# Back-to-back score halves and two shared PSUM banks in an attention and mixture-of-experts kernel

## The chip, the cores and the metric

The kernel runs on one core of a Trainium2 chip. The metric is the device time of one execution in microseconds (us); lower is better. The engines are named as in the profile: PE (TensorE; PEld is its weight loading), DVE (VectorE), ACT (ScalarE), POOL (GpSimd) and SP (SyncE, which only issues DMAs here).

## The reference

Sliding-window attention with a linear position bias, 8 sequences of 576 tokens, 8 heads of 64, then a mixture of experts in which each token takes only its best expert.

```python
# q, k, v: [8, 8, 576, 64] fp32
scores = q @ k^T / 8 - slope[h] * |i - j|        # 0 <= i - j < 128, else masked
attn   = exp(scores - max) ;  attn /= attn.sum() + 1e-9
x      = (attn @ v) as [4608, 512]               # tokens x (heads * 64)
logits = x @ w_gate                              # [4608, 8]
e      = argmax(logits) ;  g = softmax(logits)[e]
out    = g * (relu(x @ w1[e]) @ w2[e])           # w1 [8, 512, 1024], w2 [8, 1024, 512]
```

## The kernel before, in words

**Two stages.** The attention stage works through 36 chunks of 128 query rows, all 8 heads each, and writes rows and gates to a scratch tensor `xd` in HBM; a small routing computation goes on beside it. The expert stage then gathers each expert's rows from `xd` and runs the two layers. This study is about the attention stage.

**A chunk** passes through ten pieces of work, numbered `k` in `do`:

| k | what it is | engines |
|---|---|---|
| 0, 4 | scores of the first, the second four heads (`scores`): bias by a bf16 matmul, then q times k, into the two-bank tile `s0_ps` or `s1_ps`; in 64x64 tiles of the array | PE |
| 2, 5 | `weigh` of the first, the second four heads: `copy_predicated` folds the window, `tensor_reduce` takes the maximum, four exponentials with their sums go to `pe` | DVE, then ACT |
| 1, 6 | `transposes` of the first, the second four heads into one PSUM bank, a copy of it to `pT`, two masks by `affine_select` | PE, ACT, POOL |
| 7, 8 | value products (`av`) into one PSUM bank `x_ps` | PE |
| 9 | `copy_x`: that bank to `xT` | ACT |
| 3 | `rows`: `xT` times identity and gate weights into `r_ps` (two banks), scaled to `x_sb` by DVE, written to `xd`; the logits `lg` | PE, DVE, SP |

Below, S0 and S1 stand for the two score halves, T0 and T1 for the two transposes, A for the value products and R for the rows' matmuls.

**What sets the order.** Nothing is scheduled by a planner here: inside `manual_schedule` every engine runs its instructions in the order in which the code issues them. That order comes from steps. `LAGS[None][k]` says how many steps after step 4·chunk piece `k` is issued, so four steps are one period, in which one chunk's worth of each piece is issued, from five different chunks. Inside a step the pieces are sorted by the key in `step`. Before, a period c is, for PE: S0 of chunk c, T0 of c-1, R of c-4, T1 of c-1, S1 of c, A of c-2.

**Chunks differ.** In each nine chunks the first and the sixth begin a sequence (called narrow below: only one key block, so their scores are 128 instead of 192 columns wide, they have no fold, and A has half as many matmuls); the fifth is a tail of two sequences, whose A before is issued in two halves, one on each side of S1. So periods whose chunk c-2 is narrow (7, 11, 16, 20, 25, 29 and so on) have half an A.

**PSUM.** Eight banks: four for `s0_ps` and `s1_ps`, one for the transposes (`ps_t`), one for the value products (`ps_x`), two for `r_ps`.

**Routing.** After each group of chunks (`GROUPS`) a generator `route` goes through five stages, one in each period: 1 the maximum and the one-hot of the expert; 2 small matmuls on PE that count ranks, put into spare columns of `r_ps` by `spare`, and DVE work on them; 3 and 4 DVE work; 5 index matmuls on PE, again into `r_ps`. They are issued at the end of a step with s % 4 == 3, right behind A; for the groups at chunks 21, 27 and 30 `PACE` names the steps itself. Stage 3 of the group at chunk 21 also calls `shift_late`, which has one small matmul into `r_ps`.

**Weights.** From step `FETCH` on, `round_half` (a cast on ACT) and `rest_half` (a subtraction on POOL) split the first expert's weights, half a block a period.

Of the kernel before, what the change touches and what calls it, by code (L numbers as in the profile page):

```python
# [9 lines left out]
F32 = mybir.dt.float32  # L10
# [6 lines left out]
PSUM = bass.MemoryType.PSUM  # L17
# [14 lines left out]
def keep(tc, ins):  # L32
    return ins if HELD[0] else tc.keep_in_program_order(ins)


def attention(ctx, tc, st, qT, kT, v, iw, load_c2, chunk_done, chunks, begun):
# [5 lines left out]
    ptp = ctx.enter_context(tc.tile_pool(name="a_pt", bufs=2))  # L42
    xp = ctx.enter_context(tc.tile_pool(name="a_x", bufs=2))
    ps_s = ctx.enter_context(tc.tile_pool(name="ps_s", bufs=1, space=PSUM))
    ps_t = ctx.enter_context(tc.tile_pool(name="ps_t", bufs=1, space=PSUM))
    ps_x = ctx.enter_context(tc.tile_pool(name="ps_x", bufs=1, space=PSUM))
    ps_r = ctx.enter_context(tc.tile_pool(name="ps_r", bufs=1, space=PSUM))
    st["ps_x"], st["ps_t"], st["ptp"] = ps_x, ps_t, ptp

    batch = {}  # L50
    blocks = {}
# [2 lines left out]
    def score_banks():  # L54
        turns.append(turns.pop(0))
        return turns[-1]
# [60 lines left out]
                                          start=True, stop=True))  # L117

    def warm_up(n):
        w_ps = ps_x.tile([128, 512], F32, name="x_ps")  # L120
        for _ in range(n):
            keep(tc, nc.tensor.matmul(out=w_ps, lhsT=warm[:, 0:128], rhs=warm, start=True, stop=True))

    def early(op):
        bank = score_banks()[:, 0] if op not in "zog" else None
        st["early"][0](op, bank if bank is None else bank.rearrange("p a b -> p (a b)"))

    k0 = load_k(0, (0, KCUT, 320, S))
    next(k0)
# [68 lines left out]

    def transposes(subs, g, pe, pT):
        m, tail = subs[0][1] // 4, is_tail(subs)  # L200
        t_ps = ps_t.tile([128, 4, 128], F32, name="t_ps")
        for j in range(4):
            nc.tensor.transpose(out=t_ps[:, j, :], in_=pe[:, 4 * g + j, :], identity=ident)  # L203
        cut = lambda kb: pT[:, kb, 4 * g:4 * g + 4, :]
        nc.scalar.copy(out=cut(1), in_=t_ps)
        if tail:
            part = lambda ap: ap.rearrange("p h (a q) -> p h a q", a=2)
            pat = lambda k: [[0, 4], [0, 2], [k, 64]]
        else:
            part = lambda ap: ap  # L210
            pat = lambda k: [[0, 4], [k, 128]]
        if m > 0:
            nc.gpsimd.affine_select(out=part(cut(0)), in_=part(cut(1)), pattern=pat(-1), base=0,
                                    channel_multiplier=1, compare_op=ALU.is_gt, fill=0.0)
            nc.gpsimd.affine_select(out=part(cut(1)), in_=part(cut(1)), pattern=pat(1), base=0,
                                    channel_multiplier=-1, compare_op=ALU.is_ge, fill=0.0)
# [53 lines left out]
    live, pes, sums, pTs, xTs, xps, second = {}, {}, {}, {}, {}, {}, {}  # L270

    def copy_x(ch):
        xTs[ch] = xp.tile([128, NP, 128], F32, name="xT", bufs=3)
        nc.scalar.copy(out=xTs[ch], in_=xps.pop(ch))

    def do(k, ch):
        if k == 9:
            return copy_x(ch)
        subs = chunks[ch]
        if k in (0, 4):  # L280
            if k == 0:
                pes[ch] = pp.tile([128, H, 128], F32, name="pe")
                sums[ch] = small.tile([128, H], F32, name="rsum", bufs=8)
            live[ch] = scores(subs, k // 4)
        elif k in (2, 5):
            second[ch] = weigh(k // 3, pes[ch], sums[ch], *live.pop(ch), later=k == 5 and ch == len(chunks) - 1)
        elif k == 1:
            pTs[ch] = ptp.tile([128, 2, H, 128], F32, name="pT")
            transposes(subs, 0, pes[ch], pTs[ch])
            if second.get(ch):  # L290
                second.pop(ch)()
        elif k == 3:
            rows(ch, subs, xTs.pop(ch), sums.pop(ch))
        elif k == 6:
            transposes(subs, 1, pes.pop(ch), pTs[ch])
        elif k == 7:
            xps[ch] = ps_x.tile([128, NP, 128], F32, name="x_ps")
            av(subs, pTs[ch], xps[ch], range(NP // 2))
        else:
            av(subs, pTs.pop(ch), xps[ch], range(NP // 2, NP))  # L300
            if len(lags(ch)) < 10:
                copy_x(ch)

    def step(s):
        st["step"] = s
        if s == 0:
            begun(0)
        if s == 12:
            begun(1)
        for f, b, m in ahead.get(s, ()):  # L310
            f(b, m)
        for k, ch in sorted(plan.get(s, ()), key=lambda x: (1.5 if x[0] == 9 else 4.5 if x == (6, s // 4 - 1) and s % 4 == 2 else x[0], x[1])):
            do(k, ch)
        if s < len(WU) - 1:
            warm_up(WU[s + 1])
        for k in list(st["stages"]):
            if k[1] <= s and (s in PACE[k[2]] if k[2] in PACE else s % 4 == 3):
                k[1] = s + 1
                if next(k[0], k) is k:
                    st["stages"].remove(k)  # L320
        n, i = divmod(s - FETCH, 8)
        if 0 <= n < 7 and i in (0, 3, 4, 7):
# [14 lines left out]
        step(s)  # L337


LAGS = {None: (0, 4, 0, 17, 2, 2, 5, 11, 11, 12)}  # L340
LAGS.update({ch: (0, 4, 0, 17, 2, 2, 6, 11, 11, 12) for ch in range(3)})
LAGS.update({ch: (0, 4, 0, 17, 2, 2, 5, 9, 11, 12) for ch in (4, 13, 22, 31)})
LAGS.update({33: (0, 4, 0, 15, 2, 2, 5, 11, 11), 34: (0, 4, 0, 13, 2, 2, 5, 10, 10), 35: (0, 4, 0, 10, 2, 2, 5, 8, 8)})
HAND = 152
HANDS = lambda nc: {x.engine for x in (nc.tensor, nc.vector, nc.scalar, nc.gpsimd, nc.sync)}
# [9 lines left out]
PP = 3  # L355
OS = (3,)
WN = 7
FETCH = 57
WV = (0, 1)
KCUT = 128  # L360
LAST = 2
# [5 lines left out]
TT = 6  # L367
# [58 lines left out]

def spare(st, k, n):
    if st["step"] >= FREE_T:
        return st["ps_t"].tile([128, 4, 128], F32, name="t_ps")[:, k, 0:n]
    return st["r_ps"][:, k, XW:XW + n]  # L430


# [104 lines left out]
def route_last(tc, st, lg, ch, groups):  # L537
# [8 lines left out]
    key = rp.tile([128, E], F32, name="l_key", bufs=1)  # L546
# [9 lines left out]
    rest = [r for r, *_ in st["stages"]]  # L556
    st["stages"].clear()
    st["warm"](0)
    bank = st["ps_x"].tile([128, 512], F32, name="x_ps")
    rank = bank[:, 0:E]  # L560
    nc.tensor.matmul(out=rank, lhsT=tri[:, 0, :], rhs=oh, start=True, stop=False)
    nc.tensor.matmul(out=rank, lhsT=tri[:, 1, :], rhs=prev, start=False, stop=True)
    for r in rest:
# [8 lines left out]
    s = st["rank"][:, ch:ch + 1]  # L572
# [8 lines left out]
    st["warm"](1)  # L581
    for r in rest:
        list(r)
    ip = st["ps_x"].tile([128, 512], F32, name="x_ps")[:, 0:E * TT]
    for t, lp in lps.items():
        for k in range(2):
            nc.tensor.matmul(out=ip[:, E * t:E * t + E], lhsT=lp, rhs=rr[:, k, :], start=(k == 0), stop=(k == 1))
# [676 lines left out]
```

## Time and profile before

| | us |
|---|---|
| time, median of 3 runs (650.93 to 651.36) | 651.24 |
| time of the profiled execution | 651.34 |
| its span, first to last instruction | 649.5 |
| PE busy in the span | 635.6 |
| of it, in the 429.10 us from 211.90 to 641.00 (experts) | 429.10 |
| of it, in the 172.64 us from 17.00 to 189.64 (chunks 3 to 32) | 170.20 |
| DVE, ACT, POOL busy in those 172.64 us | 135.24, 141.24, 105.71 |

The granted clock of TensorE is 0.996 over the span and 1.00 in both stretches. A busy PE is not the same as a PE at its peak: its matmuls overlap and their modelled ends cover short waits, so in the attention stage the distances between the starts of matmuls say more than the busy time does.

### The profile page before, as it was taken

Reading aid. Unit: us, or ns where it says so; the run is one execution under the profiler, and the core shown is the slowest. Engines: PE = TensorE matmul, PEld = TensorE weight load, DVE = VectorE, ACT = ScalarE, POOL = GpSimd, SP = SyncE. Lnnn points to the kernel's source line nnn. Section 1 sums busy time; section 2 is a strip of 40 time slices with the busy share of each in tenths; the row PEclk is TensorE's granted clock in tenths of the full one; section 3 lists DMA queues with packets and bytes.
Section 4 is the critical chain, followed back from the end, with each engine's and each line's share of the span. In section 5 each row is a group of like instructions: output and inputs, shape, how many; then the busy total and the mean of one; then the engine's idle time right before and its main releaser. Section 6 shows DMA issues by size and latency. Waiting matters only on the chain.

```text
span 649.5 us, 15087 instructions
## 1 busy us (share of the span) xinstructions
PE 635.6 (98%) x5683; PEld 541.4 (83%) x5683; DVE 389.8 (60%) x974; ACT 316.2 (49%) x963; POOL 302.2 (47%) x414
## 2 busy tenths in 40 slices
PE   8999999999999999999999999999999999999995
PEld 4878878787887988988889889898898888888884
DVE  5568888969889786545543663565455456355411
ACT  6877778888777424433342333334233333433311
POOL 5644657768555141066317616733760750580202
PEclk9999999999999999999999999999999999999998
DMA  8958887897645243473526325433542542543101
GB/s 312 282 162 205 208 238 233 210 292 191 196 105 116 67 154 92 163 248 102 191 98 182 103 77 174 124 89 127 156 107 96 171 124 77 179 120 132 65 0 62
DMA packets 57646, 97.91 MB, mean 151 GB/s; under 512 B 11669, under 2 KB 31765, under 8 KB 56674
## 3 DMA queue, kind: packets, MB, share of 16 engines
q1 hardware_dynamic: 49090, 76.89, 39.4%
q0 software_dynamic: 8336, 19.76, 10.7%
q8 instruction: 46, 0.75, 0.5%
q14 instruction: 30, 0.25, 0.1%
q10 hardware_dynamic: 144, 0.26, 0.1%
HBM read 77.91 MB, written 18.98 MB: 149 GB/s over the span
## 4 chain that ended last, share of the span: by engine, by line
PE 68%; DVE 0%; ACT 0%; issue 0%; POOLq 0%; POOL 0%; ACTq 0%
PE y_ps L877 32%; PE l_ps L681 30%; PE s_ps L681 2%; PE x_ps L231 1%; PE r_ps L241 1%; PE x_ps L642 1%; PE y_ps L837 1%; PE t_ps L203 1%; PE x_ps L837 0%; PE s_ps L171 0%; ACT pe L190 0%; PE s_ps L642 0%; PE s_ps L162 0%; POOLq L1030 0%; PE l_ps L653 0%
## 5 line engine op out<-in xcount | busy, mean ns | idle before, releaser
L684 ACT ACTIVATE hh<-l_ps 128x336 fp32r<-128x336 f32 (+7 forms) x104 | 46.5, 447 | 203.2 <-PE l_ps L681 202.8
L688 DVE SCALAR_TENSOR_TENSOR hl<-l_ps,hh 128x336 fp32r<-128x336 f32 (+7 forms) x104 | 52.1, 501 | 151.0 <-ACT hh L684 150.8
L661 POOL DMA_INDIRECT xg<-xd,od_idx x112 | 116.7, 1042 | 35.1 <-issue 34.5
L190 ACT ACTIVATE pe<-s_ps,nmax 128x128 f32<-128x128 f32 x288 | 102.4, 376 | 32.0 <-DVE nmax L184 22.8
L877 PE MATMUL y_ps<-wh,hh 128*128 128x512 f32 (+5 forms) x280 | 110.9, 396 | 0.0
L877 PE MATMUL y_ps<-wh,hl 128*128 128x512 f32 (+5 forms) x280 | 110.4, 394 | 0.0
L877 PE MATMUL y_ps<-wl,hh 128*128 128x512 f32 (+5 forms) x280 | 110.3, 394 | 0.0
L865 POOL DMA_INDIRECT out<-y,od_pidx x33 | 34.8, 1055 | 151.7 <-ACT y L883 145.2
L969 DVE TENSOR_TENSOR wl<-w_raw,wh 128x512 fp32r<-128x512 f32 x114 | 73.9, 690 | 31.7 <-ACT wh L965 29.6
L681 PE MATMUL l_ps<-xh,wh 128*128 128x304 f32 (+9 forms) x416 | 81.7, 318 | 0.0
L681 PE MATMUL l_ps<-xh,wl 128*128 128x304 f32 (+9 forms) x416 | 81.0, 317 | 0.0
L681 PE MATMUL l_ps<-xl,wh 128*128 128x304 f32 (+9 forms) x416 | 80.8, 316 | 0.0
L681 PEld LDWEIGHTS l_ps<-xh,wh 128*128 128x128 f32 x416 | 68.1, 189 | 8.3 <-issue 1.2
L681 PEld LDWEIGHTS l_ps<-xh,wl 128*128 128x128 f32 x416 | 66.4, 189 | 1.9
L681 PEld LDWEIGHTS l_ps<-xl,wh 128*128 128x128 f32 x416 | 66.3, 189 | 1.7
L231 PE MATMUL x_ps<-pT,v_sb 128*64 128x128 f32 (+2 forms) x1152 | 66.4, 265 | 0.1
L231 PEld LDWEIGHTS x_ps<-pT,v_sb 128*64 128x64 f32 (+1 forms) x1152 | 57.0, 137 | 9.8 <-issue 5.2
L877 PEld LDWEIGHTS y_ps<-wh,hl 128*128 128x128 f32 (+5 forms) x280 | 51.4, 184 | 13.6
L965 ACT CAST wh<-w_raw 128x1024 fp32r<-128x1024 f32 x57 | 59.5, 1044 | 4.3 <-DMA w_raw<-w 4.3
L190 ACT ACTIVATION_READ_ACCUMULATOR pe<-s_ps,nmax 128x1 f32 x288 | 61.5, 214 | 0.0
L877 PEld LDWEIGHTS y_ps<-wl,hh 128*128 128x128 f32 (+5 forms) x280 | 51.6, 184 | 11.3
L877 PEld LDWEIGHTS y_ps<-wh,hh 128*128 128x128 f32 (+5 forms) x280 | 51.4, 184 | 10.3 <-ACT hh L684 0.4
(221 smaller groups left out, 957.4 us busy)
## 6 DMA issues: line engine op xcount, KB each, us to landing
w_raw<-w SPq DMA_DIRECT2D x64, 512.0 KB, 3.8
q_sb<-qT SPq DMA_DIRECT2D x39, 256.0 KB, 5.4
xd<-x_sb SPq DMA_DIRECT2D x32, 258.0 KB, 5.0
v_sb<-v SPq DMA_DIRECT2D x32, 256.0 KB, 5.0
k_sb<-kT SPq DMA_DIRECT2D x7, 1152.0 KB, 9.3
w_n<-w SPq DMA_DIRECT2D x4, 1024.0 KB, 6.2
xg<-xd,od_idx POOLq DMA_INDIRECT x112, 3.1
xd<-x_sb SPq DMA_DIRECT2D x8, 129.0 KB, 4.3
```

Source lines behind the costliest of these rows:

```text
L190: nc.scalar.activation(out=pe[:, h, :], in_=s_ps[:, c, n, lo:lo + 128], func=AF.Exp, bias=nmax[:, 2 * c + n:2 * c + n + 1], scale=1.0, acc ...
L203: nc.tensor.transpose(out=t_ps[:, j, :], in_=pe[:, 4 * g + j, :], identity=ident)
L231: nc.tensor.matmul(out=x_ps[64 * c:64 * c + 64, p, q], lhsT=blocks["v", b, m - 1 + kb][0:kk, D * h:D * h + D], rhs=pT[0:kk, kb, h, q], sta ...
L241: nc.tensor.matmul(out=r_ps[:, p, 0:XW], lhsT=xT[:, p, :], rhs=iw_sb[:, p, :], start=True, stop=True)
L661: ins = tc.nc.gpsimd.indirect_dma_start(out=g[:, s], out_offset=None, in_=parts, in_offset=bass.IndirectOffsetOnAxis(ap=idx[:, s], axis=0),)
L681: nc.tensor.matmul(out=ps, lhsT=a[:, 128 * d:128 * d + 128], rhs=b[:, d], start=(k == 0), stop=(k == 11))
L684: nc.scalar.activation(out=hh, in_=ps, func=AF.Relu)
L688: nc.vector.scalar_tensor_tensor(out=hl, in0=ps, scalar=0.0, in1=hh.bitcast(F32), op0=ALU.max, op1=ALU.subtract)
L865: ins = nc.gpsimd.indirect_dma_start(**kw).ins
L877: nc.tensor.matmul(out=ys[t][0:n], lhsT=a[:, tl], rhs=b[:, 512:1024], start=(f == 0 and k == 0), stop=(f == 7 and k == 2))
L965: keep(tc, nc.scalar.copy(out=wh, in_=raw))
L969: keep(tc, eng.tensor_tensor(out=wl[:, sl], in0=raw[:, sl], in1=wh.bitcast(F32)[:, sl], op=ALU.subtract))
```

## The change

Five edits, all in the attention stage.

1. For chunks 3 to 32 (`PAIRED`) both score halves are issued in the first step of a period (lags 0 and 0), T0 in the second with the first `weigh` behind it (lags 5 and 1), T1 in the third, then the second `weigh`, then the rows (lags 6, 2, 14; the order inside the step is set by `rank`).
2. The rows come 14 steps after the chunk's first step in place of 17, for chunks 0 to 2 too.
3. Transposes and value products take turns in one pool of two banks (`ps_b`); the warm-up matmuls and the last spare columns use it too.
4. Both halves of a tail chunk's value products are issued in one step (the lag 9 is gone).
5. `copy_x` comes first behind S0 in its step; `FETCH` is 56 in place of 57.

```diff
-    ps_t = ctx.enter_context(tc.tile_pool(name="ps_t", bufs=1, space=PSUM))
-    ps_x = ctx.enter_context(tc.tile_pool(name="ps_x", bufs=1, space=PSUM))
+    ps_b = ctx.enter_context(tc.tile_pool(name="ps_b", bufs=2, space=PSUM))
     ps_r = ctx.enter_context(tc.tile_pool(name="ps_r", bufs=1, space=PSUM))
+    st["bank"] = bank = lambda: ps_b.tile([128, 4, 128], F32, name="b_ps")
...
     def transposes(subs, g, pe, pT):
-        t_ps = ps_t.tile([128, 4, 128], F32, name="t_ps")
+        t_ps = bank()
...
-            live[ch] = scores(subs, k // 4)
+            live[ch, k // 4] = scores(subs, k // 4)
...
-            xps[ch] = ps_x.tile([128, NP, 128], F32, name="x_ps")
+            xps[ch] = bank()
...
+    def rank(k, ch, s):
+        if ch in PAIRED and k in (5, 6):
+            return 2.4 if k == 6 else 2.6
+        return 0.5 if k == 9 else 4.5 if (k, ch) == (6, s // 4 - 1) and s % 4 == 2 else k
...
-        for k, ch in sorted(plan.get(s, ()), key=lambda x: (1.5 if x[0] == 9 else 4.5 if x == (6, s // 4 - 1) and s % 4 == 2 else x[0], x[1])):
+        for k, ch in sorted(plan.get(s, ()), key=lambda x: (rank(*x, s), x[1])):
...
-LAGS = {None: (0, 4, 0, 17, 2, 2, 5, 11, 11, 12)}
-LAGS.update({ch: (0, 4, 0, 17, 2, 2, 6, 11, 11, 12) for ch in range(3)})
-LAGS.update({ch: (0, 4, 0, 17, 2, 2, 5, 9, 11, 12) for ch in (4, 13, 22, 31)})
+PAIRED = range(3, 33)
+LAGS = {None: (0, 5, 1, 14, 0, 2, 6, 11, 11, 12)}
+LAGS.update({ch: (0, 4, 0, 14, 2, 2, 6, 11, 11, 12) for ch in range(3)})
...
-FETCH = 57
+FETCH = 56
```

The line numbers of the changed kernel are 1 to 6 higher than those before. First place: PE in period 11, a period with half an A. Before (line 171 is the q-times-k part of S0 and S1, 203 the transposes, 241 the rows, 231 the value products):

```order
L171 MATMUL s0_ps_107<-k_sb_565,q_sb_763 64x192 x8
L203 MATMUL t_ps_1189<-c2_sb_64,pe_1076 128x128 x4
L241 MATMUL r_ps_1208<-iw_sb_114,xT_1097 128x144 x4
L203 MATMUL t_ps_1218<-c2_sb_64,pe_1076 128x128 x4
...
L171 MATMUL s1_ps_108<-k_sb_565,q_sb_763 64x192 x8
L231 MATMUL x_ps_1250<-pT_1090,v_sb_1072 64x128 x8
```

The same period in the changed kernel:

```order
L172 MATMUL s0_ps_104<-k_sb_574,q_sb_772 64x192 x8
...
L172 MATMUL s1_ps_105<-k_sb_574,q_sb_772 64x192 x8
L204 MATMUL b_ps_1221<-c2_sb_64,pe_1093 128x128 x4
L204 MATMUL b_ps_1238<-c2_sb_64,pe_1093 128x128 x4
L242 MATMUL r_ps_1256<-iw_sb_111,xT_1204 128x144 x4
L232 MATMUL b_ps_1266<-pT_1121,v_sb_1089 64x128 x8
```

S1 has moved up to S0, T1 to T0, and the rows now stand directly ahead of the value products.

Second place: ACT in one period. Before, the second line's `xT` copy and the cast `wh` lie between copies of the transposes (`pT`) and exponentials (`pe`):

```order
L205 COPY pT_1837<-t_ps_1838 128x512
L274 COPY xT_1846<-x_ps_1803 128x512
L190 ACTIVATE pe_1823,rsum_1824<-s0_ps_107,nmax_1849 128x128 x4
L205 COPY pT_1837<-t_ps_1869 128x512
L981 CAST wh_1779<-w_raw_1433 128x512
L190 ACTIVATE pe_1823,rsum_1824<-s1_ps_108,nmax_1894 128x128 x4
```

In the changed kernel:

```order
L275 COPY xT_1859<-b_ps_1820 128x512
L986 CAST wh_1771<-w_raw_1431 128x512
L206 COPY pT_1876<-b_ps_1877 128x512
L191 ACTIVATE pe_1845,rsum_1846<-s0_ps_104,nmax_1886 128x128 x4
L206 COPY pT_1876<-b_ps_1893 128x512
L191 ACTIVATE pe_1845,rsum_1846<-s1_ps_105,nmax_1902 128x128 x4
```

The `xT` copy and the cast have moved ahead of both `pT` copies, so the run from the first `pT` copy to the last exponential holds nothing else.

Third place: PE in period 31, where `PACE` puts routing stage 2 into the third step. Before, S1 (its last rows are the first two) lies between the rows and the first rank matmul (`tri` is a triangle of ones):

```order
L241 MATMUL r_ps_3361<-iw_sb_114,xT_3237 128x144 x4
L203 MATMUL t_ps_3372<-c2_sb_64,pe_3214 128x128 x4
...
L171 MATMUL s1_ps_108<-k_sb_2479,q_sb_2916 64x192 x2
L171 MATMUL s1_ps_108<-k_sb_2920,q_sb_2918 64x192 x2
L459 LDWEIGHTS tri_169
L459 MATMUL r_ps_3361<-oh_3296,tri_169 128x48
```

In the changed kernel:

```order
L204 MATMUL b_ps_3366<-c2_sb_64,pe_3223 128x128 x4
L204 MATMUL b_ps_3382<-c2_sb_64,pe_3223 128x128 x4
L242 MATMUL r_ps_3400<-iw_sb_111,xT_3351 128x144 x4
L465 LDWEIGHTS tri_166
L465 MATMUL r_ps_3400<-oh_3306,tri_166 128x48
```

The rank matmuls now follow the rows at once, in the same tile `r_ps`; the single matmul of `shift_late` stands likewise behind the rows of period 32.

More of the change, by code (lines that the diff above doesn't have):

```diff
@@ L44, in attention @@
     ps_s = ctx.enter_context(tc.tile_pool(name="ps_s", bufs=1, space=PSUM))
-    ps_t = ctx.enter_context(tc.tile_pool(name="ps_t", bufs=1, space=PSUM))
-    ps_x = ctx.enter_context(tc.tile_pool(name="ps_x", bufs=1, space=PSUM))
+    ps_b = ctx.enter_context(tc.tile_pool(name="ps_b", bufs=2, space=PSUM))
     ps_r = ctx.enter_context(tc.tile_pool(name="ps_r", bufs=1, space=PSUM))
-    st["ps_x"], st["ps_t"], st["ptp"] = ps_x, ps_t, ptp
+    st["bank"] = bank = lambda: ps_b.tile([128, 4, 128], F32, name="b_ps")
+    flat = lambda ap: ap.rearrange("p a b -> p (a b)")
+    st["ptp"] = ptp
     batch = {}
@@ L119, in warm_up @@
     def warm_up(n):
-        w_ps = ps_x.tile([128, 512], F32, name="x_ps")
+        w_ps = flat(bank())
         for _ in range(n):
@@ L124, in early @@
     def early(op):
-        bank = score_banks()[:, 0] if op not in "zog" else None
-        st["early"][0](op, bank if bank is None else bank.rearrange("p a b -> p (a b)"))
+        half = score_banks()[:, 0] if op not in "zog" else None
+        st["early"][0](op, half if half is None else flat(half))
     k0 = load_k(0, (0, KCUT, 320, S))
@@ L283, in do @@
                 sums[ch] = small.tile([128, H], F32, name="rsum", bufs=8)
-            live[ch] = scores(subs, k // 4)
+            live[ch, k // 4] = scores(subs, k // 4)
         elif k in (2, 5):
-            second[ch] = weigh(k // 3, pes[ch], sums[ch], *live.pop(ch), later=k == 5 and ch == len(chunks) - 1)
+            second[ch] = weigh(k // 3, pes[ch], sums[ch], *live.pop((ch, k // 3)), later=k == 5 and ch == len(chunks) - 1)
         elif k == 1:
@@ L428, in spare @@
     if st["step"] >= FREE_T:
-        return st["ps_t"].tile([128, 4, 128], F32, name="t_ps")[:, k, 0:n]
+        return st["bank"]()[:, k, 0:n]
     return st["r_ps"][:, k, XW:XW + n]
@@ L558, in route_last @@
     st["warm"](0)
-    bank = st["ps_x"].tile([128, 512], F32, name="x_ps")
-    rank = bank[:, 0:E]
+    rank = st["bank"]()[:, 0, 0:E]
     nc.tensor.matmul(out=rank, lhsT=tri[:, 0, :], rhs=oh, start=True, stop=False)
@@ L583, in route_last @@
         list(r)
-    ip = st["ps_x"].tile([128, 512], F32, name="x_ps")[:, 0:E * TT]
+    ip = st["bank"]()[:, 0, 0:E * TT]
     for t, lp in lps.items():
```

## The prediction

> **What bounds the kernel now.** I read the page's busy times first, then the busy times by stretch (its columns are duration, then busy time and count of PE, PEld, DVE, ACT and POOL, granted clock, DMA share, GB/s).
>
> ```profile
> PE 635.6 (98%) x5683; PEld 541.4 (83%) x5683; DVE 389.8 (60%) x974; ACT 316.2 (49%) x963; POOL 302.2 (47%) x414
> 17.00:189.64 172.64, 170.20 (x2710) 139.36 (x2708) 135.24 (x342) 141.24 (x596) 105.71 (x174) 1.00 0.79 215
> 211.90:641.00 429.10, 429.10 (x2493) 375.95 (x2493) 224.84 (x555) 147.94 (x259) 172.17 (x190) 1.00 0.39 122
> ```
>
> The experts, the last row, are full of matmuls and untouched: whatever the attention stage gains or loses goes straight into the end. Of the attention stage I take the stretch from S0 of chunk 3 to S0 of chunk 33, 30 periods of 5.75 us on average. PE bounds it too, with DVE and ACT at some 80%. Its busy share hides two things, so I read distances between starts in a timeline of PE: one period, S0 to the next routing matmuls.
>
> ```profile
> 126.31 0.36 PE L162 MATMUL s_ps<-bias_sb,eye_sb 64*64 64x384 bf16 x4
> ...
> 127.24 0.66 PE L203 MATMUL t_ps<-c_sb,pe 128*128 128x128 f32 x4
> 127.73 1.15 PE L241 MATMUL r_ps<-iw_sb,xT 128*128 128x144 f32 x8
> 128.72 0.60 PE L203 MATMUL t_ps<-c_sb,pe 128*128 128x128 f32 x4
> 129.25 0.36 PE L162 MATMUL s_ps<-bias_sb,eye_sb 64*64 64x384 bf16 x4
> ...
> 130.18 1.97 PE L231 MATMUL x_ps<-pT,v_sb 128*64 128x128 f32 x32
> 132.08 0.30 PE L506 MATMUL r_ps<-rr,lp 128*128 128x48 bf16 x5
> ```
>
> S takes .93, T0 .49, R .99, T1 .53, S1 .93, A 1.90: 5.77 us without a wait. The shape after the line number (64*64, 128*128, 128*64) is the tile of the array, and a change of shape has a price:
>
> ```profile
> 19.46 0.66 PE L203 MATMUL t_ps<-c_sb,pe 128*128 128x128 f32 x4
> ...
> 20.05 0.33 PE L231 MATMUL x_ps<-pT,v_sb 128*64 128x128 f32 x2
> ```
>
> The same four T matmuls take .49 to the first R (no change of shape, 127.24 to 127.73) and .59 to the first A here: a switch costs about .09 (.59 less .49, rounded down, since other joints give slightly less).
>
> **The change part by part.** Everything is worked out against the profiled execution, 651.34 us; the median of the runs is .10 lower, so no correction is needed.
>
> *One switch less.* A plain period switches at S0-T0, T1-S1, S1-A and A-S0, four times. Afterwards S0-S1 and T0-T1-R are of one shape, and S1-T0, R-A and A-S0 are left. 26 periods have the plain form (30 less chunk 3's and the three with a tail's A, whose two halves already had another order): 26 x .09 = **-2.3**. A plain period becomes 5.77 - .09 = 5.68.
>
> *The transposes' bank.* Before, T1 writes the bank that ACT must first copy out for T0. In the waits of PEld in 17:189.64 (idle us, times, largest):
>
> ```profile
> PEld t_ps L203 <- ACT pT L205: 5.3, 13, 0.7
> ```
>
> T1 now has another bank, and the copy ACT owes for it is that of the A before, over 2 us old: **-5.3**. But what is late next?
>
> *S1 behind the exponentials.* S1 of the next chunk refills `s1_ps`, which ACT's four second exponentials must have read. Before, T0, R and T1 lay between; now S1 comes straight behind S0. The loop from one S1 to the next consists of S1 to T0 (.93, as above), T0 to its copy, that copy, four exponentials, T1's copy, three more exponentials to the start of the last, and that one's release of S. ACT's rows of that period, and the one place where S before waits for exponentials:
>
> ```profile
> 127.99 0.59 ACT L205 COPY pT<-t_ps 128x512 f32<-128x512 f32 x1 [0.35 <-PE t_ps L203]
> 128.47 0.59 ACT L274 COPY xT<-x_ps 128x512 f32<-128x512 f32 x1
> 129.48 0.37 ACT L190 ACTIVATE pe<-s_ps,nmax 128x128 f32<-128x128 f32 x1 [0.41 <-DVE nmax L184]
> ...
> 130.52 0.37 ACT L190 ACTIVATE pe<-s_ps,nmax 128x128 f32<-128x128 f32 x1
> 130.86 0.60 ACT L205 COPY pT<-t_ps 128x512 f32<-128x512 f32 x1
> 131.33 0.65 ACT L981 CAST wh<-w_raw 128x512 fp32r<-128x512 f32 x1
> ...
> 11.71 0.37 ACT L190 ACTIVATE pe<-s_ps,nmax 128x128 f32<-128x128 f32 x1
> ...
> 12.22 0.36 PE L162 MATMUL s_ps<-bias_sb,eye_sb 64*64 64x384 bf16 x4 [0.84 <-ACT pe L190]
> ```
>
> That is .93 + .75 (127.24 to 127.99) + .48 + 1.38 (129.48 to 130.86) + .47 (130.86 to 131.33) + 1.04 (129.48 to 130.52) + .51 (11.71 to 12.22) = **5.56 us**. The `xT` copy and the cast are out of this loop by the order shown above. Against PE's 5.68 it is hidden with .12 to spare; so short periods no longer gain. Two kinds are shorter, by these rows:
>
> ```profile
> 95.82 1.09 PE L231 MATMUL x_ps<-pT,v_sb 128*64 128x128 f32 x16
> 96.84 0.36 PE L162 MATMUL s_ps<-bias_sb,eye_sb 64*64 64x384 bf16 x4
> 106.38 0.30 PE L162 MATMUL s_ps<-bias_sb,eye_sb 64*64 64x256 bf16 x4
> 107.05 0.33 PE L231 MATMUL x_ps<-pT,v_sb 128*64 128x128 f32 x2
> ```
>
> Half an A takes 1.02 in place of 1.90: PE needs 5.68 - .88 = 4.80, and S1 waits .76 in periods 7, 20 and 29, and .40 in 11 and 16, where ten index matmuls (132.08, some .36) fill the gap. (25 is counted below.) A narrow S takes .67 in place of .93: with it as the next S0 PE needs 5.42, S1 waits .14, behind 4, 17, 22 and 26. Sum 3 x .76 + 2 x .40 + 4 x .14 = **+3.6**.
>
> *Routing stage 2.* In periods 8, 13, 18 and 24 DVE does its stage 2 between the rank matmuls behind A and the fold of the next chunk (`COPY_PREDICATED`):
>
> ```profile
> 84.79 0.36 PE L162 MATMUL s_ps<-bias_sb,eye_sb 64*64 64x384 bf16 x4
> 56.43 0.20 DVE L465 TENSOR_TENSOR pick<-r_ps,oh 128x40 f32<-128x40 f32 x1 [1.36 <-PE r_ps L463]
> 58.40 0.70 DVE L181 COPY_PREDICATED s_ps<-mask_sb,s_ps 128x512 f32<-128x512 uint32 x1
> 84.89 0.20 DVE L465 TENSOR_TENSOR pick<-r_ps,oh 128x40 f32<-128x40 f32 x1 [1.36 <-PE r_ps L463]
> 86.12 1.02 DVE L471 TENSOR_TENSOR run<-run 128x8 f32<-128x8 f32 x1
> 88.22 0.70 DVE L181 COPY_PREDICATED s_ps<-mask_sb,s_ps 128x512 f32<-128x512 uint32 x1 [0.28 <-PE t_ps L203]
> 115.07 0.20 DVE L465 TENSOR_TENSOR pick<-r_ps,oh 128x40 f32<-128x40 f32 x1 [0.61 <-PE r_ps L463]
> 116.53 0.69 DVE L181 COPY_PREDICATED s_ps<-mask_sb,s_ps 128x512 f32<-128x512 uint32 x1
> 118.04 0.37 ACT L190 ACTIVATE pe<-s_ps,nmax 128x128 f32<-128x128 f32 x1 [0.32 <-DVE nmax L184]
> 85.86 1.27 POOL L986 TENSOR_TENSOR wl<-w_raw,wh 128x512 fp32r<-128x512 f32 x1
> ```
>
> `pick` starts .10 behind S0 (84.79, 84.89); to the fold it is 1.97, 3.05 (3.33 less the idle .28) and 1.46. I take the mean, 2.16, and the ends for the range. Fold to exponentials is 1.51 (116.53 to 118.04), so these start S0 + 3.77; by the loop above ACT would be ready at S0 + .84 + .93 + .75 + .48 = 3.00. They, and the next S1, are .77 late: +.65 in period 19 (less the .12 spare), +1.53 in 25 (half an A; includes its .76). Narrow chunks 9 and 14 have no fold (.70 less) and .52 less in front by two narrow S; with a loop of 5.30 against 5.42 they come out at +.47 each. Together **+3.1**; at 1.46 it is +.8, at 3.05 +6.7.
>
> *Rank matmuls behind R.* In periods 31 and 32 the rank matmuls and that of `shift_late` now follow R at once, in the tile that DVE is still reading:
>
> ```profile
> 104.52 0.29 PE L241 MATMUL r_ps<-iw_sb,xT 128*128 128x144 f32 x1
> 105.70 0.82 DVE L246 TENSOR_TENSOR x_sb<-r_ps,rinv 128x64 f32<-128x64 f32 x2 [0.69 <-PE r_ps L241]
> 196.41 0.26 PE L506 MATMUL r_ps<-rr,lp 128*128 128x48 bf16 x4 [0.49 <-DVE x_sb L246]
> ```
>
> From R's start to the end of `x_sb` it is 2.00; PE would go on after .99. The last row shows such a wait. A stands behind it: 2 x 1.0 = **+2.0** (0 if DVE were done, +4.8 if DVE were late by a fold and a maximum, .7 each as at 116.53).
>
> *The rest.* Behind chunk 33, R goes ahead of S1 but T1's waits go: +.1, within 1 either way. Rows sooner only advance SP's and DVE's work, at a DMA share of .79 with PE waiting for no transfer of them; the earlier cast lies in ACT's gap behind S0, and costs up to .6 (its .65) where that gap is gone. Chunks 0 to 2: 0.
>
> Sum: -2.3 - 5.3 + 3.6 + 3.1 + 2.0 + .1 = +1.2, or **652.5 us**. The change gives back nearly all that it wins.
>
> **The rivals.**
> *Stage 2 is quick.* If `pick` to fold takes 1.46 everywhere, as at 115.07, 2.3 goes: 650.2. For it: only one of the three pairs of rows is far off. Against: the subtractions on POOL, one a period from 14 on, move closer to S0. It decides at about 1.5 us.
> *Stage 2 is slow.* At 3.05 everywhere: +3.6, 656.1. For it: the row at 86.12 took 1.02 us for 8 columns while POOL's subtraction of 85.86 ran for 1.27. [...]
> *The loop is shorter than PE's period.* If the loop of 5.56 closed in 4.80, both terms for S1 go (-6.7): 645.8, faster. For it: each of its seven pieces comes from another place, and the exponentials could start sooner if T0 does. Against: .76 would have to go, and no piece shows such slack. It decides at 4.8.
>
> **How the numbers follow.** About 0.2% (1.3 us) can be told from no change: faster is below 649.9, slower above 652.5. The forecast (.50) lies close to the upper bound, its pieces uncertain by some 2 us: slower .25, same .21, faster .04. Quick stage 2 (.22): same .11, faster .11. Slow stage 2 (.16): slower. Short loop (.12): faster. Together faster .27, same .32, slower .41. The range, 648.8 to 655.5, takes in the first two cases with the bounds of the rest and half of the third; the short loop and the other half are left out.
>
> **What would show it.** In the changed profile: S1 waiting for ACT's `pe` by about .76 in periods with half an A; no wait of the transposes for `pT`; plain periods of 5.68 us; S1 late by .65 to 1.5 behind stage 2, with `pick` to fold near 2.2; two waits of about 1 us for `x_sb` in periods 31 and 32. S1 waiting in every plain period would mean that the loop is longer than PE's period, some .1 each 26 times, and that the forecast is too low; a wait of A for POOL's masks, of which I count none, likewise.

## The result and the profile after

| | before | changed |
|---|---|---|
| time, median of 5 runs each, us | 651.24 (650.86 to 651.72) | 659.51 (655.65 to 659.81) |
| ratio, 95% interval | | 1.0107 (1.0088 to 1.0125) |
| time of the profiled execution, us | 651.34 | 655.65 |
| its span, us | 649.5 | 653.9 |
| from S0 of chunk 3 to S0 of chunk 33 | 172.64 | 176.30 |
| from there to the full stretch of the experts | 22.26 | 23.53 |

The changed kernel is slower by about 1.1%, and its executions scatter: two of the five took about 656 us at a mean granted clock of 0.997, three about 659.6 at 0.994. The profile is of the fastest of them, so it explains 4.3 us of the change, and the other 4 us of the median have to come from something that not every execution has.

The busy times of the changed kernel by stretch, the three stretches that answer to those of before (duration, then PE, PEld, DVE, ACT, POOL, clock, DMA share, GB/s):

```profile
17.08:193.38 176.30, 168.32 (x2717) 144.56 (x2716) 139.72 (x348) 140.63 (x597) 105.73 (x177) 1.00 0.78 211
193.38:216.91 23.53, 20.26 (x311) 15.89 (x309) 18.52 (x55) 15.15 (x61) 9.73 (x16) 1.00 0.39 94
216.91:646.00 429.09, 429.09 (x2493) 375.71 (x2493) 224.40 (x551) 147.91 (x259) 171.87 (x189) 1.00 0.39 121
```

The experts take 429.09 us as before, so all of it is the attention stage: +3.66 in the 30 periods, +1.27 behind them, while the rest of the span came out .6 shorter. The 30 periods are not quite the same work: with the rows three steps sooner, R of chunk 0 falls into period 3 (5.97 us in place of 4.95), so that the stretch holds the rows of 30 chunks (240 matmuls) in place of 29 (232), and one R less comes behind it. About 1.0 of the +3.66 is this moved work. PE was idle for 2.4 us of the 30 periods before and is for 8.0 now. The waits of PE in these periods (us in all, times, longest):

```profile
PE s_ps L163 <- ACT pe L191: 5.2, 9, 0.9
PE r_ps L465 <- DVE x_sb L247: 1.2, 2, 0.9
PE r_ps L522 <- DVE x_sb L247: 0.9, 1, 0.9
```

The transposes' wait for `pT` (before, 2.2 us in this view and 5.3 in that of PEld) is gone from both. In its place stand the two waits that the prediction had named: the scores (line 163 is the bias part that opens S0 and S1) for the exponentials, and the rank and shift matmuls for `x_sb`. In the timeline of PE, a plain period, one behind half an A, and one behind the routing of the group at chunk 15:

```profile
126.89 0.36 PE L163 MATMUL s_ps<-bias_sb,eye_sb 64*64 64x384 bf16 x4
...
127.73 0.33 PE L163 MATMUL s_ps<-bias_sb,eye_sb 64*64 64x384 bf16 x4
...
128.64 1.10 PE L204 MATMUL b_ps<-c_sb,pe 128*128 128x128 f32 x8
129.57 1.15 PE L242 MATMUL r_ps<-iw_sb,xT 128*128 128x144 f32 x8
130.65 1.97 PE L232 MATMUL b_ps<-pT,v_sb 128*64 128x128 f32 x32
132.55 0.30 PE L163 MATMUL s_ps<-bias_sb,eye_sb 64*64 64x256 bf16 x4
...
44.91 0.36 PE L163 MATMUL s_ps<-bias_sb,eye_sb 64*64 64x384 bf16 x4
...
46.58 0.36 PE L163 MATMUL s_ps<-bias_sb,eye_sb 64*64 64x384 bf16 x4 [0.66 <-ACT pe L191]
...
114.20 0.36 PE L163 MATMUL s_ps<-bias_sb,eye_sb 64*64 64x384 bf16 x4 [0.34 <-ACT pe L191]
...
116.09 0.36 PE L163 MATMUL s_ps<-bias_sb,eye_sb 64*64 64x384 bf16 x4 [0.88 <-ACT pe L191]
```

The plain period takes 132.55 - 126.89 = 5.66 us (5.68 forecast) and waits for nothing. S1 of chunk 8 comes 1.67 behind its S0 in place of .84, after half an A. In period 20 both halves wait, S0 for .34 and S1 for .88: DVE's routing work in front of the fold of chunk 19 has made the exponentials of that chunk 1.6 us late.

**By period.** Taking each of the 30 periods against the shortest one of its kind in the traces (5.65 plain, 4.78 with half an A, 5.12 with a narrow S0, and what routing matmuls add), the changed kernel loses 11.3 us in them. Without this it would take 165.0, and 164.0 without the moved R. That is 8.6 below the 172.64 of before: the 2.3 and 5.3 that the prediction removes, and 1.0 more, for which it has no term. The tails' value products in one piece (edit 4), which it counted at nothing, take 1.1 out of the same stretch by themselves (tail, below).

| lost to | forecast | measured | in periods |
|---|---|---|---|
| the loop of S1 behind the exponentials | 3.6 | 3.8 | 8, 21, 30 (.84 each), 5, 12, 17, 18, 23 (.2 to .3 each) |
| DVE's routing work | 3.1 | 4.6 | 19, 20, 24 to 28 (.2 to 1.1 each) |
| S0 of chunk 16, cause open | 0 | .6 | 15 |
| rank and shift matmuls behind `x_sb` | 2.0 | 2.4 | 31, 32 (1.0 each), 11, 16 (.2 each) |
| behind chunk 33 | .1 | 1.3 | |

(A period is counted from S0 to S0, so that what half an A does to S1 shows in the period behind it. The loss in period 15 is not DVE's: S0 of chunk 16 starts at 91.23, and the last exponential that had to read its bank started at 88.72. This period takes 5.95 to 7.22 us in the profiles of the paired kernels with the same work in it, and the views put S0's wait down to another instruction in each of the changed kernel's profile, exfirst and pace.)

### The profile page after: what moved, and what is told of

It is laid out like the page before. It is cut to its first block, busy times and chain, and to the rows that moved or that the text cites. A ratio compares the mean times of both kernels' runs of the same rounds, so it can differ in the third digit from the quotient of the medians.

```text
span 653.9 us, 15061 instructions
## 1 busy us (share of the span) xinstructions
PE 632.1 (97%) x5683; PEld 544.7 (83%) x5683; DVE 392.6 (60%) x974; ACT 315.3 (48%) x963; POOL 299.6 (46%) x414
## 4 chain that ended last, share of the span: by engine, by line
PE 71%; ACT 2%; DVE 2%; issue 0%; POOLq 0%; POOL 0%; ACTq 0%; DVEq 0%
PE y_ps L882 32%; PE l_ps L686 30%; PE b_ps L232 2%; PE s_ps L686 2%; ACT pe L191 1%; PE r_ps L242 1%; PE b_ps L204 1%; PE s_ps L172 1%; PE x_ps L647 1%; PE y_ps L842 1%; DVE x_sb L247 0%; PE s_ps L163 0%; ACT pT L206 0%; PE x_ps L842 0%; DVE nmax L185 0%
## 5 line engine op out<-in xcount | busy, mean ns | idle before, releaser
L232 PE MATMUL b_ps<-pT,v_sb 128*64 128x128 f32 (+2 forms) x1152 | 66.1, 265 | 1.7 <-ACT pT L206 1.6
L232 PEld LDWEIGHTS b_ps<-pT,v_sb 128*64 128x64 f32 (+1 forms) x1152 | 57.1, 136 | 9.3 <-issue 2.8
L191 ACT ACTIVATION_READ_ACCUMULATOR pe<-s_ps,nmax 128x1 f32 x288 | 64.8, 225 | 0.0
L882 PEld LDWEIGHTS y_ps<-wl,hh 128*128 128x128 f32 (+5 forms) x280 | 51.5, 184 | 11.3
```

What stands on the lines that cost most here:

```text
L191: nc.scalar.activation(out=pe[:, h, :], in_=s_ps[:, c, n, lo:lo + 128], func=AF.Exp, bias=nmax[:, 2 * c + n:2 * c + n + 1], scale=1.0, acc ...
L232: nc.tensor.matmul(out=x_ps[64 * c:64 * c + 64, p, q], lhsT=blocks["v", b, m - 1 + kb][0:kk, D * h:D * h + D], rhs=pT[0:kk, kb, h, q], sta ...
L882: nc.tensor.matmul(out=ys[t][0:n], lhsT=a[:, tl], rhs=b[:, 512:1024], start=(f == 0 and k == 0), stop=(f == 7 and k == 2))
```

## The experiments

Each kernel was timed in five rounds beside the kernel before on the same chip; ratios are to that one. The chips differ by up to 2.6 us in the median of before (651.1 to 653.7), so ratios are compared, and in profiles the stretch from S0 of chunk 3 to S0 of chunk 33.

### Again, the old order with the new banks, and two parts undone

The changed kernel once more:

> The changed kernel as it is, for the spread of its executions (two of five took about 656 us, three about 659.6, at a mean granted clock of 0.997 and 0.994) and for a second profile. If the 4 us are a lower granted clock in one stretch, a profile of a 659.6 us execution shows one stretch with a clock under 1.00 and the same waits as the first. If they are a wait that comes about in some executions, the clock is 1.00 in every stretch and one or more waits of PE have grown by 4 us together.

Then the banks alone, the order of before kept:

```diff
-PAIRED = range(3, 33)
-LAGS = {None: (0, 5, 1, 14, 0, 2, 6, 11, 11, 12)}
-LAGS.update({ch: (0, 4, 0, 14, 2, 2, 6, 11, 11, 12) for ch in range(3)})
+PAIRED = ()
+LAGS = {None: (0, 4, 0, 17, 2, 2, 5, 11, 11, 12)}
+LAGS.update({ch: (0, 4, 0, 17, 2, 2, 6, 11, 11, 12) for ch in range(3)})
-FETCH = 56
+FETCH = 57
```

> The order of before (S1 in the third step, T1 in the second, rows 17 steps behind), with the two shared banks, the copy of x first, and a tail's A in one piece. Theory 1 (the loop of S1 behind the exponentials, into which DVE's routing work passes, is what costs): T1 no longer waits, nothing is put behind the exponentials, so 646 to 648 us. Theory 2 (sharing the two banks makes transposes and value products wait for each other): 651 us or more, with waits of T1 or A for ACT in the profile.

The same with the rows 14 steps behind, `LAGS = {None: (0, 4, 0, 14, 2, 2, 5, 11, 11, 12)}`, and `FETCH` 56:

> The changed kernel with S1 and the transposes back in the steps of before, the rows still 14 steps behind and the earlier cast. Theory 1: the loop of S1 is gone, 646 to 649 us, and no wait of S1 for ACT over 0.2 us in chunks 3 to 32. If the rows that come sooner are what costs, it stays at 655 us or more while the kernel with the order of before is at 651 or less.

And two routing steps moved, `21: (122, 127, 131, 132, 135)` in `PACE`:

> The changed kernel with two of the routing steps one step later (126 to 127, 130 to 131), so that the rank matmul and the late shift's matmul stand behind the value products and not behind the rows. Both waits of 0.9 us for x_sb in periods 31 and 32 go, with what they delay: 1.8 to 2.2 us less than the changed kernel run beside it. If DVE then comes late with the fold of chunks 32 and 33, half of it comes back.

| | median, us | before beside it | ratio, 95% interval |
|---|---|---|---|
| again | 659.41 (657.55 to 665.28) | 653.30 | 1.0106 (1.0074 to 1.0138) |
| banks | 651.88 (651.55 to 652.44) | 653.30 | 0.9978 (0.9968 to 0.9988) |
| unpair | 670.60 (668.99 to 671.93) | 653.30 | 1.0256 (1.0238 to 1.0274) |
| pace | 660.29 (657.63 to 664.21) | 653.30 | 1.0107 (1.0081 to 1.0133) |

**Banks** came out between the two theories in time, and its wait is the one that theory 2 names. From the waits of PEld in its profile, from 17 to 188 us:

```profile
PEld b_ps L204 <- ACT xT L275: 3.9, 9, 0.7
```

T1 now takes the bank of the last value products, which ACT copies out in front of T0's copy: most of the wait (5.3 before) is still there, only for another copy, and 1.4 more of T's waits are put down to other work of ACT. About half of the .2% comes from the tails (see "tail" below; in the 30 periods the two kernels take 171.48 and 171.55 us). So in the old order the bank removes little; the 5.3 us went with bank and order together, and the new order with one bank was not run.

**Unpair** was missed by over 20 us, and it does not isolate the rows: with T1 directly behind T0 and ahead of the rows, T1 comes about a microsecond sooner, and this wait grows (from 15 to 200 us):

```profile
PEld b_ps L204 <- ACT xT L275: 16.9, 20, 1.7
```

Whether sooner rows cost anything is answered by lag18 below.

**Pace** took out what was expected of periods 31 and 32 (.97 us each, from their lengths), and gave more back in period 33, which grew from 8.4 to 11.6 us. The wait of A there in its timeline, and the busy times by stretch around it (the ninth column is the granted clock):

```profile
198.67 0.59 PE L232 MATMUL b_ps<-pT,v_sb 128*64 128x64 f32 x6 [2.88 <-ACT pT L206]
```

```profile
196.00:200.00 4.00, 1.33 (x22) 1.25 (x23) 3.77 (x12) 2.47 (x10) 0.00 (x0) 0.81 0.01 2
200.00:208.00 8.00, 8.00 (x93) 6.79 (x92) 2.98 (x12) 3.77 (x18) 2.69 (x4) 0.50 0.40 90
```

For 8 us behind the wait TensorE ran at half its clock (.50 from 200 to 208 us). The changed kernel's own profile has the same wait of A in period 33, 1.6 us long, and ACT's instructions show where it comes from:

```profile
198.92 0.30 PE L232 MATMUL b_ps<-pT,v_sb 128*64 128x64 f32 x3 [1.59 <-ACT pT L206]
```

```profile
196.80 0.37 ACT L191 ACTIVATE pe<-s_ps,nmax 128x128 f32<-128x128 f32 x1 [2.72 <-DVE c L500]
...
198.18 1.08 ACT L206 COPY pT<-b_ps 128x512 f32<-128x512 f32 x2
```

The four exponentials of chunk 33 come first, and both copies of the transposes of chunk 32 behind them; A takes over the bank of the first of these transposes, so the shared banks (edit 3) have a part in this wait.

The wait and the clock behind it are one cause for executions to differ. **Again** showed a second: its period 11 took 7.46 us in place of 5.32, at a clock of 1.00.

```profile
68.61 0.66 PE L232 MATMUL b_ps<-pT,v_sb 128*64 128x128 f32 x8 [2.26 <-DMA v_sb<-v]
```

A waited for a value block. In the first profile of the changed kernel the same block was issued at 57.06, took 9.1 us and landed at 66.15, .14 us ahead of its use. SP's queue says why it is late. Before:

```profile
50.70 0.42 SPq L61 DMA_DIRECT2D k_sb<-kT  x1
...
57.49 1.61 SPq L534 DMA_DIRECT2D xd<-gate  x3
```

In the changed kernel:

```profile
52.52 2.26 SPq L540 DMA_DIRECT2D xd<-gate  x3
...
55.94 0.42 SPq L62 DMA_DIRECT2D k_sb<-kT  x1
56.45 0.55 SPq L1202 DMA_DIRECT2D xd<-x_sb  x1
57.06 0.64 SPq L75 DMA_DIRECT2D v_sb<-v  x1
```

Routing starts a period sooner with the rows, so the first group's gate writes now stand ahead of the key load of the next sequence (1,152 KB), which SP issued at 55.94 in place of 50.70, with one write of rows between it and the value block.

### The key load, the routing steps, the rows, and POOL's subtraction

Four changes to the changed kernel, each by itself. The key loads one step sooner (`KA = 17` in place of 16, and never ahead of step 0):

> The changed kernel with the loads of the keys one step sooner, so that on SP's queue the key load of sequence 2 stands ahead of the gate writes of the first routing group (in the changed kernel it stood behind them, was issued at 55.94 in place of 50.70, and the value block of chunk 9 issued after it landed .14 us before its use in one execution and 2.2 us late in another). If that is what scatters the changed kernel, the wait of A in period 11 is below 0.1 us, the value block lands 2 us or more ahead of its use, and executions that were 2 us apart for this reason come together: 0 to 2 us less in the median. If the wait comes from elsewhere (a slow DMA whatever stands ahead of it), it shows in some executions as before.

The routing steps of the group at chunk 21, `21: (119, 123, 127, 131, 135)`:

> The changed kernel with the routing steps of the group at chunk 21 at 119, 123, 127, 131 and 135, behind the value products, which the earlier rows allow. Theory 1 (DVE's routing work in front of a fold delays ACT, and PE waits; two waits of 0.9 us for x_sb in periods 31 and 32, 1.6 us or more of A in period 33): the two waits go (-2), and the routing work of 2.9 us that stood ahead of the fold of chunk 33 is spread, so that A of period 33 waits under 0.5 us and the halved clock behind that wait (0.50 from 200 to 208 us in the kernel with two routing steps later) does not come: 4 us or more less than the changed kernel, 2.5 us from the earlier routing being the least. If the wait in period 33 is not DVE's, it stays.

The rows a period later, `LAGS = {None: (0, 5, 1, 18, 0, 2, 6, 11, 11, 12)}`:

> The changed kernel with the rows a whole period later (18 steps in place of 14), at the same place of a period. Routing and its writes then come as late as in the kernel before. If the rows' being sooner is what costs (SP's order, the first routing steps), 2 to 4 us less than the changed kernel and no wait of A in period 11. If it is the loop and DVE's work in it, which move along by a period, it stays within 1.5 us of the changed kernel.

And POOL's subtraction replaced:

```diff
-        nc.gpsimd.tensor_tensor(out=wl[:, sl], in0=raw[:, sl], in1=wh.bitcast(F32)[:, sl], op=ALU.subtract)
+        nc.gpsimd.memset(wl.bitcast(F32)[:, sl], 0.0)
```

> The changed kernel with POOL's subtraction for the first expert's weights replaced by a memset of the same tile; the low part of these weights is left out (zero), and POOL reads nothing there. Theory 1, port form: DVE's routing instructions that took 1.0 to 1.15 us while the subtraction ran (run at 109.29, t at 146.05, oh at 139.07) come down to 0.2 to 0.4, and the waits of S for ACT in periods 20, 26 and 27 shrink by 3 us together. Rival, amount form (the routing work is too much for the gap even when it runs free): those waits shrink by less than 1 us.

| | median, us | before beside it | ratio, 95% interval |
|---|---|---|---|
| klead | 658.47 (658.39 to 660.71) | 653.66 | 1.0090 (1.0073 to 1.0107) |
| pace2 | 657.58 (656.87 to 663.29) | 653.66 | 1.0087 (1.0058 to 1.0117) |
| lag18 | 660.45 (660.25 to 660.74) | 653.66 | 1.0105 (1.0090 to 1.0120) |
| nolock | 656.84 (655.09 to 658.26) | 653.66 | 1.0056 (1.0042 to 1.0071) |

**Nolock** comes out near theory 1: its 30 periods take 173.28 us, 3.0 less (.3 of it in period 15, which varies by itself), and the waits of S for ACT fall from 5.2 to 3.0. They did not all fall where expected: periods 19, 20, 24, 25 and 28 are .4 to .8 shorter, 26 and 27 are not. DVE's instructions in front of the fold of chunk 19 and POOL's beside them, in the changed kernel:

```profile
108.20 0.20 DVE L471 TENSOR_TENSOR pick<-r_ps,oh 128x40 f32<-128x40 f32 x1 [0.92 <-PE r_ps L469]
...
109.29 1.15 DVE L477 TENSOR_TENSOR run<-run 128x8 f32<-128x8 f32 x1
...
110.58 0.45 DVE L481 TENSOR_SCALAR t<-rank 128x5 f32<-128x5 f32 x1
...
111.14 0.69 DVE L182 COPY_PREDICATED s_ps<-mask_sb,s_ps 128x512 f32<-128x512 uint32 x1
...
109.14 1.27 POOL L991 TENSOR_TENSOR wl<-w_raw,wh 128x512 fp32r<-128x512 f32 x1
110.38 0.62 POOL L70 TENSOR_SCALAR q_sb<-q_sb 128x512 f32<-128x512 f32 x1
```

and with the memset:

```profile
108.64 0.17 DVE L477 TENSOR_TENSOR run<-run 128x8 f32<-128x8 f32 x1
...
108.94 0.57 DVE L481 TENSOR_SCALAR t<-rank 128x5 f32<-128x5 f32 x1
...
109.62 0.69 DVE L182 COPY_PREDICATED s_ps<-mask_sb,s_ps 128x512 f32<-128x512 uint32 x1
...
108.37 0.53 POOL L991 MEMSET wl<- 128x512 f32 x1
108.86 0.62 POOL L70 TENSOR_SCALAR q_sb<-q_sb 128x512 f32<-128x512 f32 x1
```

An addition over 128x8 takes 1.15 us while POOL subtracts and .17 beside a memset; `t` is slow beside POOL's scaling of q in both (.45 and .57, against .17 at 186.84 in the changed kernel, without that scaling). The memset reads no tile, and it is also shorter (.53 against 1.27), so the run does not show which of the two makes the difference; but the addition begins while it still runs (at 108.64, the memset ending at 108.90) and is not held up.

**Lag18** (the rows of chunks 0 to 2 stay where they are) settles the rows: a period later the ratio is the same, 1.0105. Its executions lie within .5 us of each other, and period 11 (5.05) has no wait. Of the eight profiles with paired scores, rows 14 steps behind and the key load at its old step, three have this wait of A (2.26, 2.08 and 1.70 us in again, exfirst and seam); lag18 and the three with the sooner key load (klead, combo, seamk) have none. So sooner rows, by way of SP's order, do cause the scatter's first part; but later rows move the routing to other periods and lose as much there (periods 16 and 17 took .5 and .9 more than in the changed kernel). **Klead** has period 11 at 5.32, which by itself proves little, since the first profile of the changed kernel had that too; two of its five executions are still 2 us longer than the others at a clock of .991, and these have another cause. Its profile, too, has a clock of .57 from 200 to 204 us, behind the wait of A in period 33. **Pace2** takes 2.1 us out of periods 31 and 32, but A still waits 1.6 us in period 33, and the expectation failed in its second half. The wait is still behind DVE's routing work: with the steps moved, stage 4 of the same group (`eq` and `rr`, 191.71 to 193.78) stands in front of the fold of chunk 33, which starts 2.14 us behind S0 in place of 1.61.

### The loop, the seam at chunk 33, and the tails

The second weigh ahead of T1, which moves nothing on PE and puts T1's copy behind the second exponentials on ACT:

```diff
-            return 2.4 if k == 6 else 2.6
+            return 2.8 if k == 6 else 2.6
```

> The changed kernel with the second weigh ahead of T1 in its step, so that ACT does the second four exponentials ahead of T1's copy; nothing else moves, PE's order is the same. Theory 1 (the loop from one S1 to the next through ACT is 5.59 us, T1's copy being .47 of it): the loop becomes 5.12, every wait of S1 behind ACT shrinks by up to .47, the half-A periods (5.59 from S1 to S1) come down by about as much, and there are some ten such periods: 3 to 5 us less than the changed kernel up to the S0 of chunk 33. Rival (ACT's exponentials are late only because of DVE, and T1's copy is in a gap): less than 1 us.

Chunk 33, the first that is not paired, with its first weigh a step later, `33: (0, 4, 1, 15, 2, 2, 5, 11, 11)`:

> The changed kernel with the first weigh of chunk 33 one step later, behind T0 of chunk 32, as it stands in the paired chunks. In the changed kernel ACT has the exponentials of chunk 33, late by DVE's routing work, ahead of both copies of the transposes of chunk 32; A waits for one of them, 1.6 us in its profile, 2.9 us in another, where the clock fell to half behind it. Theory 1: that wait goes, S0 33 to S0 34 comes down from 8.4 us by about 1.5, and so does the scatter: no execution more than 2 us above the lowest, 2 to 5 us less in the median. If the wait for DVE only moves to the next piece, it stays at 8 us or more, and the scatter too.

The kernel before, with its `LAGS` line of the chunks 4, 13, 22 and 31 taken out:

> The kernel before with the value products of the tail chunks in one piece (the lag 9 is gone), and nothing else: two switches of shape less in each of four periods, .2 us each. Together with the waits of T1 there, 1 to 1.5 us less than before, as much as the kernel with the shared banks in the old order gained; then the banks in themselves gained nothing.

And the four mends exfirst, seam, pace2 and klead together in the changed kernel:

> The changed kernel with four mends together: the second exponentials first, chunk 33's first weigh one step later, the routing steps of the group at chunk 21 earlier, and the key loads one step sooner. By theory 1 the sum of their parts against the changed kernel's 655.7 to 659.7 us: 3 to 5 (loop), 2 to 5 (wait of A in period 33 and the halved clock), 2 (waits for x_sb): 647 to 651 us on a chip where before takes 651.2, a ratio of .993 to 1.000. If the stalls only change places, it stays at 1.005 or more.

| | median, us | before beside it | ratio, 95% interval |
|---|---|---|---|
| exfirst | 653.18 (651.20 to 654.74) | 652.90 | 0.9999 (0.9988 to 1.0011) |
| seam | 658.64 (657.15 to 659.81) | 652.90 | 1.0086 (1.0072 to 1.0100) |
| tail | 651.68 (650.96 to 653.38) | 652.90 | 0.9988 (0.9979 to 0.9997) |
| combo | 650.11 (649.41 to 650.98) | 652.90 | 0.9958 (0.9945 to 0.9971) |

**Exfirst** is the strongest single answer: one number in `rank`, PE's order untouched, and the whole loss of the changed kernel is gone. Its 30 periods, the waits of S in them, and one wait that is not the loop's:

```profile
16.62:189.69 173.07, 166.74 (x2718) 143.98 (x2716) 130.65 (x349) 140.69 (x597) 104.84 (x175) 1.00 0.80 216
```

```profile
PE s_ps L163 <- ACT pe L191: 1.3, 4, 0.4
```

```profile
67.17 1.09 PE L232 MATMUL b_ps<-pT,v_sb 128*64 128x128 f32 x16 [2.08 <-ACT pe L191]
```

176.30 - 173.07 = 3.2 us less, though this execution had the long wait of A in period 11 (the view puts it down to ACT; in the profile of seam the same matmul's 1.70 are put down to the value block's DMA). Without it, 5.2. Behind them, period 33 came down from 8.40 to 7.67. The loop was that of the prediction, and .47 less of it is worth more than the 3.6 that the prediction had put on the short periods: 24, 25, 27 and 28, which lose by DVE's routing work, came down too, by .3 to .6 each, so a part of DVE's lateness passes through the same loop.

**Seam** took period 33 from 8.4 to 6.74 us and its executions had a clock of .998 or .999, but 1.3 came back in period 34, and the value block's wait is there (1.70): 2.7 us of scatter, and .1 to .2% in the median by the ratios, where 2 to 5 us were expected. **Tail** gained .12%, about half of what banks did, and the intervals touch; its profile is shorter by 1.1 us at S0 of chunk 33 (171.55 against 172.64). **Combo** runs below both kernels, as the sum of its parts said, with 169.31 us in the 30 periods, 3.3 under before with one R more in them.

### What the scatter is

> The changed kernel a third time, for a profile of an execution 4 us above the lowest. Two causes are open: the value block of chunk 9 that lands late (A of period 11 waits 2.1 us, clock 1.00), and the clock that falls to half behind the wait of A in period 33 (a mean clock .003 lower). Executions with a mean clock of .997 or more and 2 us or more above the lowest speak for the first, executions with .994 or less for the second; a profile with period 11 at 7.4 us or with a clock under .9 between 198 and 208 us shows it.

> The changed kernel with both sources of the scatter mended: the key loads one step sooner and chunk 33's first weigh one step later. If these two are the scatter, its executions lie within 1.5 us of each other at a mean clock of .997 or more, near the lowest of the changed kernel beside it, and its profile shows period 11 at 5.3 us and no clock under .9 from 190 to 215 us. The stalls that are the same in all executions (loop, DVE's routing, two waits for x_sb, 11 us by the first profile) stay: a ratio of 1.005 to 1.008. If scatter remains, its cause is another.

| | median, us | before beside it | ratio, 95% interval |
|---|---|---|---|
| again2 | 657.78 (657.16 to 658.40) | 651.06 | 1.0099 (1.0084 to 1.0114) |
| seamk | 655.50 (654.47 to 656.76) | 651.06 | 1.0066 (1.0054 to 1.0079) |

The profiled execution of again2 took 658.40 us. Its stretch behind A's wait, and the same stretch of the first profile of the changed kernel (655.65 us):

```profile
201.00:205.00 4.00, 4.00 (x65) 3.00 (x66) 1.51 (x9) 2.20 (x10) 0.20 (x2) 0.57 0.69 136
```

```profile
201.00:205.00 4.00, 4.00 (x72) 3.35 (x72) 2.71 (x12) 2.82 (x14) 1.48 (x2) 1.00 0.35 86
```

A waited 1.6 us in both; behind it the clock fell to .57 in the one and stayed at 1.00 in the other, and periods 33 and 34 took .73 and .69 more. So 1.4 of the 2.75 us between these two executions is the clock, and 1.0 was lost in periods 0 to 2, for a reason that no run here shows. Seven profiles have a wait of 1.6 us there: in two (klead, again2) the clock fell, and period 33 took 9.32 and 9.13 us; in five (after, again, nolock, lag18, pace2) it stayed at 1.00, and in all of these but pace2 (8.93) the period is 8.4. So a wait of 1.6 us is followed by a lower clock in some executions and not in others; what decides it is not shown. The clock does not sort all executions of again2, though: two at .994 took 658.40 and 657.85, two at .997 took 657.72 and 657.16.

With both sources mended (seamk) the value block landed at 62.85, 3.5 us ahead of its use at 66.35, period 33 took 6.74 us, and all six executions had a clock of .997 or .998. The scatter is 2.3 us, more than the 1.5 expected, and the kernel .33% faster than the changed one beside it. What stays is the 11 us that all executions lose in common.

On the first chip, where the changed kernel took 659.6 us three times, no profile of such an execution exists. The two causes seen are worth 2.1 us (value block) and 1.4 us or more (clock), and its clock of .994 speaks for the second at least; that the two together make the 4 us there remains an inference.

## Why the prediction was wrong

**Forecast and rivals.** 652.5 was forecast, with a range to 655.5; the median is 659.5, and even the fastest execution, 655.65, lies outside. Of the rivals, slow stage 2 (656.1) comes nearest in time and names a part of the cause: `pick` to fold took 2.94 and 2.38 us where the fold follows (108.20 to 111.14, 144.83 to 147.21), 2.16 having been counted. The short loop is refuted: where DVE is on time it closes in 5.6 us (S1 of chunk 16 to S1 of chunk 17: 92.06 to 97.67).

**Right.** What is removed: a plain period of 5.66 against 5.68, and no wait of the transposes (for which the bank needed the new order, as banks shows). The loop behind the exponentials, 3.8 against 3.6. The two waits of PE for `x_sb` in periods 31 and 32, 2.0 of each.

**Mis-sized: "Routing stage 2", 3.1 against 4.6.** The step counted the rank stage alone, in periods 8, 13, 18 and 24, and took its price from the kernel before. The loss came after 19 and in a row from 24 to 28, where stages 1, 3 and 4 stand in front of a fold too (`oh` of stage 1 took 1.14 us at 139.07). In the new order DVE does routing work in front of the next fold, and POOL's subtractions fall into the same place; that the order of before absorbed a late fold between its two score halves is argued, not measured. Nolock took some 2.7 us of it away. The narrow chunks 9 and 14, for which .47 each were counted, lost nothing.

**Failed: "The rest".** "Rows sooner only advance SP's and DVE's work" is the step that went wrong in kind. Routing began a period sooner, its gate writes went ahead of a key load on SP's queue, the key load came 5 us later, and a value block behind it lands with .14 us to spare, or, in three profiles, 1.7 to 2.3 us too late. The sentence had argued from the DMA share, where SP's order shows it. Undoing this step alone (lag18) gained nothing all the same, since the routing work then cost as much elsewhere. And "+.1 behind chunk 33" overlooked the seam; 1.3 was measured, with one R less to do there. Chunk 33 keeps the old lags, so ACT has its exponentials, late by routing work, ahead of two copies of the transposes of chunk 32, and A waits 1.6 us for the first of them; behind this wait the clock fell to .57 in two profiles (klead, again2) and stayed at 1.00 in five.

**The sum** thus missed by 2.6 in the 30 periods (1.5 routing, .6 the wait in period 15, .4 `x_sb`, .2 the loop; the moved R of 1.0 and the gain of the tails, about as large, cancel), by 1.2 behind them, less .6 elsewhere, and by some 4 through a scatter that the median holds and the sum had no term for; what makes up these 4 us on that chip is inferred from the other chips' profiles, not shown.

## What to carry to other kernels

Here, with PE and ACT near their bound (busy for 168.32 and 140.63 of 176.30 us), a wait that was removed at one instruction reappeared at the next: in the old order the second bank left most of the wait in place (3.9 of 5.3 us), and the new order then put DVE's lateness into a loop with hardly any slack (5.56 us forecast, against 5.66 of a plain period). Close the loop first (which instruction of the next round waits for which of this one, over which engines, and how long is each piece), and take out of it whatever need not be there: here .47 us of copy were worth the whole loss. When a piece moves, write down the order of every DMA queue before and after, and the lead of each transfer over its use; a lead of .14 us was a scatter between executions here. And when pieces move across the bounds of the stretch that is compared, count the work in it on both sides.

## What was not expected of the hardware

- A wait of 1.6 us of PE was followed by a TensorE clock of .57 over 4 us in two profiles (klead, again2) and by 1.00 in five others; one of 2.88 us by .50 over 8 us (pace).
- An addition of 128x8 on DVE took 1.15 us beside a subtraction of 128x512 on POOL (changed kernel) and .17 beside a memset (nolock).
- A transfer of 256 KB issued 1.1 us behind one of 1,152 KB took 9.1 us to land (changed kernel), and 6.0 where the larger one was issued 5.2 us ahead (seamk).
